# Delta-rule prelude on one core: the second block's Grams behind the first Y, weight tiles loaded one by one

## The chip, the cores and the metric

The kernel runs on one core of a Trainium2 chip. Measured is the device time of one execution in microseconds (us), and the median over several runs is compared. One execution of the kernel before was also taken with the hardware profiler; every row below comes from it. The engines are named as in the profile: TensorE is PE (its weight loads PEld), VectorE is DVE, ScalarE is ACT, GpSimd is POOL, and SyncE (SP) only issues transfers.

## What is computed

Four batches of eight heads run a delta rule over 768 steps with head dimension 48; the result, 3072 tokens of 384 values, goes through two weight matrices with a clipped square between them. 

```python
k_n = k / (np.linalg.norm(k, axis=-1, keepdims=True) + 1e-06)
for t in range(S):
    kt, vt, bt = (k_n[:, :, t], v[:, :, t], beta[:, :, t, None])
    y[:, :, t] = np.einsum('bhd,bhde->bhe', q[:, :, t], state)
    v_old = np.einsum('bhde,bhd->bhe', state, kt)
    state = state + bt[:, :, :, None] * np.einsum('bhd,bhe->bhde', kt, vt - v_old)
...
h = x @ w_in                                   # (3072, 384) @ (384, 2048)
g = np.where(h >= 1, h, np.where(h <= -1, 0.0, (h + 1) ** 2 / 4))
return g @ w_out                               # (3072, 2048) @ (2048, 384)
```

## The kernel before, in words

**Blocks.** The 768 steps are cut into 12 chunks of 64. Two chunks make a pair G (`NS` = 6 pairs), and one chunk of all 32 heads is a block g of 32 triangular 64×64 problems, two heads stacked on the 128 partitions (`NU` = 16 columns of units). For each block the kernel forms the Gram of its keys (`gram_k`, or `gram_first` for the first two), solves (I + A)⁻¹ and gets the output Y and the new state.

**The solve.** For blocks 0 and 1 the diagonal 16×16 parts are inverted on VectorE, one problem per lane (`lanes16`, `solve16`, `unlanes16`, lines 348 to 419); TensorE then joins 16s to 32s (`merge16_a`, `merge16_b`) and 32s to 64s (`merge32_a`, `merge32_b`, lines 431 to 512), `chain_u` applies the inverse to the values, and `first_y` forms the first block's Y. Each of these steps is a batch of small matmuls and then evictions, and waits for the one before it.

**The Grams.** `gram_first(g)` (line 255) does not compute 64×64 Grams but three 32×32 quarters of each, 96 matmuls; its main part leaves the diagonal quarters in PSUM as VectorE reads them, and `below` lets ScalarE copy the third. `gram_k` (line 244) computes whole 64×64 Grams in 32 matmuls. Every one of these matmuls is of type f32 and runs in two passes: the trace shows a weight load and a matmul for each pass. `gram_q(g)` (line 274, 32 matmuls) forms the products of keys and queries; its `evict` is four ScalarE copies onto `WQ`, and GpSimd masks them.

**The weights.** `w_in` and `w_out` come in 16 tiles (`wt`, 768 KB each), loaded by `weight_loads` from SP's queue, the first eight (`SOON`) at the start. The loaded words have to be taken apart: `parts` (line 188) is two ScalarE instructions for each tile (lines 192, 194), `words` (line 198) one VectorE instruction. The second matmul of an item needs its tile whole.

**The order.** The engines run their own lists in order, and the order in which the Python code issues work is that list. From line 686 the prelude is written out by hand: both `gram_first`, both `gram_q`, `hold(KEEP)` (line 675: matmuls on zeros whose result nobody reads, 13 of 256 columns, 26 passes), VectorE's solve of block 0, the merges by `step`, which may put `hold` matmuls (`HEAT`) ahead of a step's evictions, then `first_y`. The generator `bg` (`aside`) carries VectorE's solve of block 1; `pu` and `wu` carry `parts` and `words`.

**The item loop** (from line 916) takes one weight tile at a time for a pair: `up` (x @ w_in into `h`, line 751), ScalarE's and VectorE's activation (lines 904, 932, 940), and `down` (line 770). The pair G = 0 starts with block 0 alone, while block 1 is still in its merges. Tables say what is done between the items: `FIRST`, `OPEN`, `SECOND`, `STEADY` give the slot of each step of the chain in units of half items, `BACK`, `GAIT` and `PACE` how many steps of `bg`, `pu` and `wu` follow each half item.

The queue order at the start is: SP issues the K and Q tiles of both blocks (ScalarE's queue takes six of them), weight tiles 0 and 1, the KV tiles of both blocks and weight tiles 2 to 7.

Of the kernel before, what the change touches and what calls it, by code (L numbers as in the profile page):

```python
# [23 lines left out]
KEEP = 13  # L24
# [10 lines left out]
def delta_rule_moe(ctx: ExitStack, tc: tile.TileContext, kqa, kqb, kv, beta, w, out):  # L35
# [56 lines left out]
    def first_w():  # L92
        tiles = [(g, i) for g in range(2) for i in range(NT)]
        for t in tiles:
            WK[t] = sb.tile([P, NV, C], F32, name="WK", bufs=4)
            WQ[t] = sb.tile([P, 2, NV, C], F32, name="WQ", bufs=4)
        for g, i in tiles:
            nc.sync.dma_start(out=WK[g, i][0:D], in_=kqb[g, i][0:D, 0])
            nc.scalar.dma_start(out=WK[g, i][C:C + D], in_=kqa[g, i][:, 0])
        for g, i in tiles:  # L100
            nc.sync.dma_start(out=WQ[g, i][0:C, 1], in_=kqb[g, i][:, 2])
            (nc.sync if g else nc.scalar).dma_start(out=WQ[g, i][C:C + D, 0], in_=kqa[g, i][:, 1])
# [12 lines left out]
    first_w()
# [671 lines left out]

    FIRST = {'ln': [9.5, 9.5, 10.0, 11.0, 10.0, 10.5, 10.5], 'so': [11.0, 15.0], 'un': [15.5, 15.5, 17.0, 17.0], 'va': [12.0, 15.5], 'vb': [20.0, 19.5], 'r': [16.0], 'm': [17.5, 17.5, 19.0, 19.0], 'kt': [18.0], 'K': [20.0, 20.5], 'T': [21.5, 22.0, 23.0, 23.5, 24.5, 25.0, 25.5], 'Q': [28.5, 29.0]}
    OPEN = {'M': [6.0, 7.0, 7.5, 8.0, 1.0], 'I': [8.5, 9.5, 10.0, 10.5, 2.0, 9.0, 13.0, 14.0], 'X': [1.5, 2.0, 2.5, 4.0, 4.0, 6.5, 6.5, 6.5], 'L': [10.5, 13.5, 4.5], 'W': [23.5, 0.5]}
    SECOND = {'ln': [-6.0, -6.0, -6.0, -5.5, -5.0, -5.5, -5.0], 'so': [-5.0, 4.0]}  # L790
# [1 line left out]
    PACE = [1, 1, 0, 0, 1, 0, 1, 0, 1, 0, 1, 0, 1, 0, 1, 0, 1, 0, 0, 1, 2, 0, 1, 0, 1, 0, 1, 1]
# [1 line left out]
    GAIT = [0, 1, 0, 1, 1, 2, 1, 1, 0, 4, 1, 1, 1, 2, 1, 0, 2, 2, 0, 1, 0, 0, 1, 1, 1, 2]
# [204 lines left out]
```

## Time and profile before

| | |
|---|---|
| median of 3 runs | 610.52 us (610.04 to 611.68) |
| profiled execution | 610.52 us, its span 608.8 us |
[...]
| TensorE matmul busy | 572.8 us, 94% of the span |
| TensorE weight loads | 476.5 us, 78%, beside the matmuls |
| VectorE | 433.0 us, 71% |
| ScalarE | 337.4 us, 55% |
| GpSimd | 61.6 us, 10% |
| the chain that ended last | TensorE 53%, "issue" 27%, VectorE 14%, ScalarE 3% |

The busy shares are means over the whole span. A busy TensorE may be at either clock, and its start is unlike its steady part: in the first two of 40 slices of the span TensorE is 60% and 70% busy, in most later ones over 90%. "Issue" is time in which an engine waited for nothing that the profile shows.

### The profile page before, as it was taken

How to read it: one execution, taken by the hardware profiler on the slowest of the kernel's cores; microseconds unless marked ns; L12 is line 12 of the kernel's file. 1: busy time of each engine (PE TensorE's matmuls, PEld its weight loads, DVE VectorE, ACT ScalarE, POOL GpSimd, SP SyncE). 2: the span in 40 equal slices, each digit the busy share in tenths (PEclk: the TensorE clock that was granted, in tenths of full speed). 3: DMA queues.
4: the chain of work that ended last, by engine and by line, in shares of the span. 5: the costliest groups of instructions: out<-in, count | busy, mean ns of one | idle time of the engine just before them, and what ended most of it. 6: DMA issues, size and time to landing. Idle time of an engine off the chain costs nothing.

```text
span 608.8 us, 19694 instructions
## 1 busy us (share of the span) xinstructions
PE 572.8 (94%) x8572; PEld 476.5 (78%) x8572; DVE 433.0 (71%) x942; ACT 337.4 (55%) x621; POOL 61.6 (10%) x91
## 2 busy tenths in 40 slices
PE   6788897999899999899998999998999999999996
PEld 5666564567677787788887888987888888898995
DVE  7358979995989987779965689955789955433332
ACT  3537883628467577457365547376546375454442
POOL 5054001300004000003000003000003000000000
PEclk8577998999999999999999999999999999999998
DMA  7928322002142000153000332000431000010001
GB/s 234 408 54 309 139 81 90 2 27 56 39 145 90 2 28 2 48 162 89 9 22 2 110 111 79 27 4 2 123 97 53 1 3 13 18 52 1 2 0 52
DMA packets 20646, 42.37 MB, mean 70 GB/s; under 512 B 4336, under 2 KB 9440, under 8 KB 20560
## 3 DMA queue, kind: packets, MB, share of 16 engines
q1 hardware_dynamic: 19440, 40.03, 20.8%
q8 instruction: 67, 1.10, 0.7%
q10 hardware_dynamic: 544, 0.79, 0.5%
q0 software_dynamic: 576, 0.30, 0.3%
q14 instruction: 19, 0.16, 0.1%
HBM read 34.31 MB, written 4.72 MB: 64 GB/s over the span
## 4 chain that ended last, share of the span: by engine, by line
PE 53%; issue 27%; DVE 14%; ACT 3%; DMA 0%; POOL 0%; SPq 0%; POOLq 0%; ACTq 0%; DVEq 0%
PE o L770 18%; PE h L754 17%; PE ch L238 7%; PE h L751 3%; DVE pr L463 2%; DVE A L465 2%; PE ch L586 2%; PE ch L486 2%; PE o L677 1%; DVE wt L204 1%; DVE A L331 1%; DVE s L940 1%; DVE wt L213 1%; DVE GG L242 1%; PE h L263 1%
## 5 line engine op out<-in xcount | busy, mean ns | idle before, releaser
L754 PE MATMUL h<-xb,wt 128*128 128x512 f32 x720 | 182.7, 398 | 1.9 <-DVE s L940 1.6
L770 PE MATMUL o<-wt,ghi 128*128 128x384 f32 x680 | 182.4, 352 | 0.0
L754 PEld LDWEIGHTS h<-xb,wt 128*128 128x128 f32 x720 | 132.6, 188 | 29.5 <-DVE s L940 2.3
L770 PEld LDWEIGHTS o<-wt,ghi 128*128 128x128 f32 x680 | 121.7, 188 | 9.8 <-issue 1.0
L770 PE MATMUL o<-wt,glo 128*128 128x384 f32 x352 | 120.1, 353 | 0.0
L940 DVE SCALAR_TENSOR_TENSOR s<-s,h 128x512 f32<-128x512 f32 (+1 forms) x89 | 58.7, 659 | 58.5 <-ACT s L932 58.1
L899 ACT CAST ghi<-s 128x512 fp32r<-128x512 f32 x80 | 49.7, 621 | 89.9 <-DVE s L940 74.7
L904 ACT ACTIVATE s<-h,half 128x512 f32<-128x512 f32 (+1 forms) x89 | 59.5, 669 | 59.4 <-PE h L754 49.8
L900 DVE TENSOR_TENSOR glo<-s,ghi 128x512 fp32r<-128x512 f32 x80 | 55.1, 689 | 43.6 <-ACT ghi L899 40.6
L770 PEld LDWEIGHTS o<-wt,glo 128*128 128x128 f32 x352 | 65.7, 188 | 3.0 <-DVE glo L900 0.3
L465 DVE TENSOR_TENSOR A<-A,pr 128x30 f32<-128x30 f32 (+9 forms) x150 | 55.1, 368 | 5.2
L932 ACT ACTIVATE s<-s 128x512 f32<-128x512 f32 (+1 forms) x89 | 54.9, 617 | 2.3
L463 DVE TENSOR_TENSOR pr<-A 128x30 f32<-128x30 f32 (+9 forms) x150 | 52.5, 350 | 3.1
L293 POOL TENSOR_SCALAR_AFFINE_SELECT WQ<-WQ 64x512 f32<-64x512 f32 x48 | 34.4, 717 | 161.7 <-ACT WQ L285 159.3
L751 PE MATMUL h<-xb,wt 128*128 128x256 f32 (+1 forms) x144 | 42.2, 430 | 1.8 <-DVE glo L940 1.1
L751 PEld LDWEIGHTS h<-xb,wt 128*128 128x128 f32 x144 | 26.9, 194 | 13.7 <-issue 3.8
L547 ACT COPY SU<-ch 64x384 f32<-64x384 f32 x44 | 20.8, 472 | 16.2 <-PE ch L238 15.5
L586 PEld LDWEIGHTS ch<-WQ,SU 112*64 112x64 f32 x704 | 22.0, 138 | 9.2 <-issue 8.1
L586 PE MATMUL ch<-WQ,SU 112*64 112x64 f32 (+1 forms) x704 | 23.4, 224 | 5.1 <-issue 5.1
L632 DVE TENSOR_TENSOR SU<-ch,SU 48x384 f32<-48x384 f32 x40 | 22.2, 555 | 7.3 <-PE ch L238 6.7
L285 ACT COPY WQ<-ch 64x512 f32<-64x512 f32 x42 | 24.4, 581 | 4.0 <-PE ch L238 3.3
L335 POOL TENSOR_SCALAR_AFFINE_SELECT A<-A 128x1024 f32<-128x1024 f32 x5 | 6.8, 1357 | 195.5 <-ACT y L300 163.5
(167 smaller groups left out, 653.4 us busy)
## 6 DMA issues: line engine op xcount, KB each, us to landing
wt<-in_w_dram SPq DMA_DIRECT2D x16, 768.0 KB, 10.6
KV<-in_kv_dram SPq DMA_DIRECT2D x24, 384.0 KB, 4.6
out_dram<-wx SPq DMA_DIRECT2D x21, 192.0 KB, 2.9
WQ<-in_kqb_dram SPq DMA_DIRECT2D x24, 128.0 KB, 2.7
WK<-in_kqb_dram SPq DMA_DIRECT2D x24, 96.0 KB, 3.5
WQ<-in_kqa_dram SPq DMA_DIRECT2D x22, 96.0 KB, 2.9
WK<-in_kqa_dram SPq DMA_DIRECT2D x20, 96.0 KB, 3.5
xb<-stg SPq DMA_DIRECT2D x60, 32.0 KB, 2.0
```

The costliest lines, as they stand in the source:

```text
L238: nc.tensor.matmul(tiles[i][dst:dst + l.shape[-1], v], l, r, start=True, stop=True)
L463: nc.vector.tensor_tensor(out=pr, in0=A[:, 0:n, j:j + 1].broadcast_to([P, n, m]), in1=A[:, j:j + 1, j + 1:32].broadcast_to([P, n, m]), op= ...
L465: nc.vector.tensor_tensor(out=A[:, 0:n, j + 1:32], in0=A[:, 0:n, j + 1:32], in1=pr, op=ALU.add)
L586: nc.tensor.matmul(yy[tk:tk + C, v // NP, v % NP], SF[rows, u:u + C], w_[rows, h, v, :], start=True, stop=True)
L751: nc.tensor.matmul(h[:, cols(bs)], W32[f][:, 0, k * P:(k + 1) * P], X32[:, k, cols(bs)], start=(k == 0), stop=(k == 2))
L754: nc.tensor.matmul(h[:, cols(bs)], WT[f][:, 0, x, k * P:(k + 1) * P], XB[G][:, y, k, cols(bs)], start=(n == 0), stop=(n == 8))
L770: nc.tensor.matmul(oacc[G, k], x[:, k * P:(k + 1) * P], y, start=(new and n == 0), stop=(left[G, b] == 0 and n == len(passes) - 1))
L899: nc.scalar.copy(out=ghi[:, c], in_=s[:, c])
L900: nc.vector.tensor_tensor(out=glo[:, c], in0=s[:, c], in1=ghi[:, c], op=ALU.subtract)
L904: nc.scalar.activation(out=out, in_=in_, func=AF.Relu, bias=bias, scale=scale)
L932: nc.scalar.activation(out=s[:, c], in_=s[:, c], func=AF.Square)
L940: nc.vector.scalar_tensor_tensor(out=s[:, c], in0=s[:, c], scalar=1.0, in1=h[:, c], op0=ALU.min, op1=ALU.max)
```

## The change

1. `gram_first` is called for block 0 alone, and block 1 gets `gram_k(1)`, issued between `first_y`'s matmuls and its evictions, into the PSUM banks `START[4:6]`. That is 64 matmuls of two passes less. The diagonal quarter that `lanes16(1)` reads is then copied by GpSimd inside the block `GG` (a new first step of `lanes16(1)`).
2. `gram_q(1)` moves from the prelude into the item loop, slot 2.5 (`OPEN["q"]`).
3. `hold(KEEP)` becomes 7 matmuls of 512 columns (14 passes) instead of 13 of 256; `HEAT` has one hold matmul ahead of `merge16_a`'s evictions, as before, none ahead of `merge16_b`'s, and one after `chain_u`'s matmuls.
4. `first_w` takes one block; at the start only block 0's K, Q, beta, KV and block 1's K are loaded. Block 1's Q, beta and KV and the K of block 2 come later.
5. `mark(f)` allocates weight tile f and lets ScalarE copy one element into it, so that the tile's load waits for that ScalarE instruction. The tiles 0 to 7 are loaded behind eight such marks.
6. `parts` runs for three tiles before `merge16_b` instead of two, and the tables `BACK`, `FIRST`, `OPEN`, `SECOND`, `PACE`, `GAIT` have other numbers.

```diff
-KEEP = 13
+KEEP = 7
...
+    def mark(f):
+        RAW[f] = const.tile([P, 2, 2 * DM], F32, name=f"wt{f}")
+        nc.scalar.copy(out=RAW[f][0:1, 0, 0:1], in_=half[0:1, 0:1])
+        weight_loads(f, f + 1)
+
+    first_w(0)
+    first_q(0)
...
     load_beta(0)
-    weight_loads(0, 2)
     load_kv(0)
-    load_kv(1)
-    weight_loads(2, SOON)
+    first_w(1)
...
+        if g:
+            F["G", 1] = GG[:, 1, :, 32:64]
+            for r in (0, C):
+                nc.gpsimd.tensor_copy(out=GG[r:r + 32, 1, :, 32:64], in_=GG[r:r + 32, 1, :, 0:32])
+            yield
...
-    HEAT = [1, 1, 0, 0, 0]
-    BACK = [0, 7, 0, 1, 2, 4, 1, 3, 0, 0, 5, 5, 1, 8, 1, 0, 13]
+    HEAT = [1, 0, 0, 0, 1]
+    BACK = [1, 0, 3, 7, 5, 2, 1, 3, 0, 1, 2, 2, 6, 5, 2, 0, 9]
...
-    ends = [gram_first(0), gram_first(1)]
+    below = gram_first()
     nc.gpsimd.memset(SF, 0.0)
-    load_beta(1)
     run(ln[0], 1)
     b16 = block16(0)
-    run(b16, 1)
+    run(b16, 2)
     run(ln[0], 1)
     run(b16)
     clear()
-    ends[1][0]()
-    ends[0][1]()
-    late_q = [gram_q(0)()]
-    late_q.append(gram_q(1)())
-    hold(KEEP)
+    mark(0)
+    below()
+    mark(1)
+    end = gram_q(0)
+    hold(KEEP, 512)
     run(ln[0])
-    ends[1][1]()
-    run(pu, 2 * HOLD)
+    end = end()
+    load_beta(1)
+    mark(2)
+    run(pu, 2)
+    mark(3)
+    run(pu, 2)
+    first_q(1)
+    mark(4)
     run(solve16(0))
     run(unlanes16(0))
     step(merge16_a, HEAT[0], ((norm16(0), 9), (sv[0], 1)))
+    run(pu, 2)
     step(merge16_b, HEAT[1])
+    mark(5)
+    load_kv(1)
     step(merge32_a, HEAT[2], ((sv[0], 1),))
-    late_q[0]()
+    end()
     step(merge32_b, HEAT[3], ((pu, 1), (wu, 1)))
-    load_k(2)
+    mark(6)
     step(chain_u, HEAT[4], ((pu, 1), (wu, 1)))
-    first_y()()
+    y = first_y()
+    spare[:] = START[4:6]
+    k1 = gram_k(1)
+    y()
+    mark(7)
+    k1()
     rest_beta()
     run(pu, 1)
-    run(bg, 2)
+    load_k(2)
     load_kt(3)
     load_q(2)
     nc.gpsimd.memset(SF[:, 2 * NU * D:], 0.0)
-    late_q[1]()
...
+            at(pe, G, OPEN["q"][0], one(gram_q, 1))
```

What this does to the lists of TensorE and ScalarE is shown at three places.

TensorE, from the start to the first merge, the kernel before (L140 the warm-up, L263 `gram_first`, L238 `gram_q`, L677 the hold, L428 `merge16_a`; x2 is two matmuls):

```order
L140 MATMUL o_121<-warm 128x128 x6
L263 MATMUL ch<-WK 32x32 x96
L263 MATMUL h<-WK 32x32 x96
L238 MATMUL o_383<-WQ,WK 64x64 x2
L238 MATMUL o_384<-WQ,WK 64x64 x2
...
L238 MATMUL o_421<-WQ,WK 64x64 x2
...
L677 MATMUL o_160<-wt_153,warm 128x256 x13
L428 MATMUL ch<-XT,wt_150 64x16 x2
```

and after the change (L269 `gram_first`, L244 `gram_q`, L684 the hold, L435 `merge16_a`):

```order
L146 MATMUL o_97<-warm 128x128 x6
L269 MATMUL ch<-WK 32x32 x96
L244 MATMUL h<-WQ,WK 64x64 x32
L684 MATMUL o_136<-wt_129,warm 128x512 x7
L435 MATMUL o_387<-XT,wt_126 64x16 x2
```

The second `gram_first` and the second `gram_q` are gone from ahead of the hold, and the hold's matmuls are twice as wide.

TensorE behind `chain_u`, after the change (L568 `first_y`, L244 on `WK` alone `gram_k(1)`, L770 the first `h`); before, `first_y` follows `chain_u` directly and the first `h` follows `first_y`:

```order
L684 MATMUL o_136<-wt_129,warm 128x256
L568 MATMUL ch<-WQ,wt_126 64x64 x2
...
L568 MATMUL ch<-WQ,KV 48x64 x4
L244 MATMUL o_659<-WK 64x64 x2
...
L770 MATMUL h<-xb 128x256 x3
```

A hold matmul now stands ahead of `first_y`, and the 32 matmuls of `gram_k(1)` between `first_y` and the first item.

ScalarE from block 0's `below` to the third tile's `parts`, after the change (L119 the marks; L273 `below`; L287 `gram_q(0)`'s evictions; L198 and L200 `parts`, of the tiles wt_254, wt_259 and wt_320, which are weight tiles 0, 1, 2; L444 `merge16_a`'s eviction):

```order
L119 COPY wt_254<-half 1x1
L273 COPY GG<-ch 32x16x32 x2
L119 COPY wt_259<-half 1x1
L287 COPY WQ<-h 64x512 x4
L119 COPY wt_320<-half 1x1
L198 ACTIVATE wt_254<-wt_254,floor 128x768
L200 ACTIVATE wt_254<-wt_254 128x768
L119 COPY wt_325<-half 1x1
L198 ACTIVATE wt_259<-wt_259,floor 128x768
L200 ACTIVATE wt_259<-wt_259 128x768
L119 COPY wt_334<-half 1x1
L444 COPY xb<-o_387 128x128
```

The marks of tiles 2, 3 and 4 stand behind `gram_q(0)`'s evictions and between the `parts` of tiles 0 and 1. Before, ScalarE had eight copies of `gram_q` in this place and the loads of all eight tiles had been issued from the start.

## Rows read from the trace of the kernel before

**Rows 1.** Busy time by stretch: stretch, length, PE, PEld, DVE, ACT, POOL, PEclk, DMA, GB/s
```profile
20.40:33.30 12.90, 10.64 (x144) 8.84 (x140) 0.00 (x1) 9.02 (x15) 0.29 (x1) 0.70 0.98 349
...
48.00:98.60 50.60, 43.82 (x807) 31.53 (x807) 43.70 (x103) 38.15 (x72) 9.32 (x13) 0.96 0.43 160
98.60:608.80 510.20, 494.50 (x6796) 414.74 (x6796) 362.57 (x754) 278.30 (x513) 34.67 (x45) 0.99 0.16 46
```

**Rows 2.** Chain of waits, first 50 us: start us, length us, what
```profile
20.70 2.26 issue
...
24.51 7.64 PE o L677 x26
32.15 0.16 PE ch L428 x2
...
42.29 0.58 issue
...
43.87 2.66 PE o L561 x86
...
48.00 2.04 PE h L751 x4
```

**Rows 3.** VectorE's timeline, 17 to 34 us: start, length, instruction, idle before and releaser
```profile
17.81 1.10 DVE L412 STREAM_TRANSPOSE XT<-xb 128x512 f32<-128x512 f32 x1
...
19.69 0.69 DVE L418 COPY wt<-xb 32x256 f32<-32x256 f32 x2
33.30 0.61 DVE L242 COPY xb<-h 64x128 f32<-64x128 f32 x2 [12.92 <-PE h L428]
```

**Rows 4.** TensorE's timeline, first 21 us
```profile
10.31 2.93 PE L263 MATMUL h<-WK 48*32 48x32 f32 x128 [2.86 <-issue]
16.78 1.39 PE L263 MATMUL h<-WK 48*32 48x32 f32 x45 [3.54 <-issue]
18.10 2.08 PE L238 MATMUL o<-WQ,WK 48*64 48x64 f32 x66
```

**Rows 5.** DMA queues, 13.2 to 16.8 us: packets, MB, share of 16 engines
```profile
q1 hardware_dynamic: 417, 1.44, 99.0%
q8 instruction: 1, 0.02, 1.6%
```

**Rows 6.** DMA queues, 78.4 to 82 us
```profile
q1 hardware_dynamic: 70, 0.33, 22.2%
q8 instruction: 1, 0.02, 1.8%
```

**Rows 7.** The hold's line alone, two stretches: length, PE, PEld, PEclk, DMA, GB/s
```profile
24.40:27.90 3.50, 3.46 (x8) 2.83 (x9) 0.50 1.01 410
27.90:32.20 4.30, 4.25 (x19) 3.35 (x18) 0.97 1.03 301
```

**Rows 8.** TensorE's timeline at 111 us, `gram_q` in a later pair
```profile
110.75 1.16 PE L238 MATMUL ch<-WQ,WK 48*64 48x64 f32 x64
```

**Rows 9.** ScalarE's timeline, first 48 us
```profile
6.01 0.20 ACT L153 ACTIVATE root<-half 128x1 f32<-128x1 f32 x1
...
20.11 2.39 ACT L285 COPY WQ<-o 64x512 f32<-64x512 f32 x4 [5.59 <-PE o L238]
...
29.66 0.98 ACT L192 ACTIVATE wt<-wt,floor 128x768 int32<-128x768 uint8 x1
30.54 0.89 ACT L194 ACTIVATE wt<-wt 128x768 f32<-128x768 f32 x1
...
42.15 0.48 ACT L539 COPY KV<-h 128x384 f32<-128x384 f32 x1 [1.01 <-PE h L238]
```

**Rows 10.** VectorE's timeline at 58 us, a Gram's two copies
```profile
57.80 1.39 DVE L242 COPY GG<-ch 64x512 f32<-64x512 f32 x2
```

**Rows 11.** GpSimd's timeline at 36 us
```profile
35.94 1.27 POOL L503 COPY XT<-XT 32x512 f32<-32x512 f32 x2 [15.26 <-DVE XT L452]
```

**Rows 12.** DMA issues of the page: KB each, us to landing
```profile
wt<-in_w_dram SPq DMA_DIRECT2D x16, 768.0 KB, 10.6
```

More of the change, by code (lines that the diff above doesn't have):

```diff
@@ L90, in load_q, with first_w, first_q @@
             nc.sync.dma_start(out=x[C:C + D, 0], in_=kqa[g, i][:, 1])
[L92 to L102, printed above, removed]
+    def first_w(g):
+        qs = (nc.sync, nc.sync if g else nc.scalar)
+        for i in range(NT):
+            WK[g, i] = sb.tile([P, NV, C], F32, name="WK", bufs=4)
+            WQ[g, i] = sb.tile([P, 2, NV, C], F32, name="WQ", bufs=4)
+            qs[0].dma_start(out=WK[g, i][0:D], in_=kqb[g, i][0:D, 0])
+            qs[1].dma_start(out=WK[g, i][C:C + D], in_=kqa[g, i][:, 0])
+    def first_q(g):
+        qs = (nc.sync, nc.sync if g else nc.scalar)
+        for i in range(NT):
+            qs[0].dma_start(out=WQ[g, i][0:C, 1], in_=kqb[g, i][:, 2])
+            qs[1].dma_start(out=WQ[g, i][C:C + D, 0], in_=kqa[g, i][:, 1])
     def load_kv(g, q=nc.sync):
@@ L110, in weight_loads @@
         for f in range(n0, n1):
-            RAW[f] = const.tile([P, 2, 2 * DM], F32, name=f"wt{f}")
+            if f not in RAW:
+                RAW[f] = const.tile([P, 2, 2 * DM], F32, name=f"wt{f}")
             nc.sync.dma_start(out=RAW[f].bitcast(I32), in_=w.bitcast(I32)[:, f])
-    first_w()
+    def mark(f):
+        RAW[f] = const.tile([P, 2, 2 * DM], F32, name=f"wt{f}")
+        nc.scalar.copy(out=RAW[f][0:1, 0, 0:1], in_=half[0:1, 0:1])
+        weight_loads(f, f + 1)
+    first_w(0)
+    first_q(0)
     beta_sb = const.tile([P, NS, 32], F32, name="beta_sb")
@@ L251, in evict, with gram_first @@
             for k, r in enumerate((0, C)):
-                copy(ONE[0][min(g // 2, 2)][k] if g > 1 else g, GG[r:r + C, g % 2, NV:NU], ts[1][C - r:2 * C - r])
+                copy(g > 1 and ONE[0][min(g // 2, 2)][k], GG[r:r + C, g % 2, NV:NU], ts[1][C - r:2 * C - r])
         return evict
-    def gram_first(g):
+    def gram_first():
         d, e = (ps.tile([P, NU, 32], F32, **acc()) for _ in range(2))
-        F["G", g] = d
+        F["G", 0] = d
         for o, c, t in ((0, 0, d), (32, 32, d), (32, 0, e)):
@@ L261, in gram_first @@
                 for tk, ft, _, h in pairs:
-                    k = WK[g, u // NV][ft:ft + D, u % NV, :]
+                    k = WK[0, u // NV][ft:ft + D, u % NV, :]
                     nc.tensor.matmul(t[tk + o:tk + o + 32, u], k[:, o:o + 32], k[:, c:c + 32], start=True, stop=True)
-        def evict():
-            F["G", g] = GG[:, g, :, 32:64]
-            nc.scalar.copy(out=F["G", g], in_=d)
         def below():
             for r in (32, C + 32):
-                nc.scalar.copy(out=GG[r:r + 32, g, :, 0:32], in_=e[r:r + 32])
-        return evict, below
+                nc.scalar.copy(out=GG[r:r + 32, 0, :, 0:32], in_=e[r:r + 32])
+        return below
     def gram_q(g):
@@ L786, in delta_rule_moe @@
     pe, fill = {}, {}
[L788 to L790 removed]
+    FIRST = {'ln': [9.5, 9.5, 9.5, 10.5, 10.0, 10.5, 10.5], 'so': [10.5, 15.5], 'un': [15.5, 15.5, 17.5, 17.5], 'va': [11.5, 14.0], 'vb': [19.0, 20.0], 'r': [15.5], 'm': [17.5, 17.5, 18.5, 18.5], 'kt': [19.0], 'K': [19.5, 20.5], 'T': [21.5, 22.0, 22.5, 23.5, 24.5, 25.0, 26.0], 'Q': [26.5, 29.0]}
+    OPEN = {'M': [6.5, 7.0, 7.5, 8.0, 1.0], 'I': [8.5, 9.5, 10.0, 10.5, 2.0, 9.0, 11.5, 13.5], 'X': [1.5, 2.5, 4.0, 5.0, 7.0, 7.0, 7.5, 7.5], 'L': [10.5, 12.0, 4.5], 'q': [2.5], 'W': [22.5, 0.5]}
+    SECOND = {'ln': [-6.0, -6.0, -5.5, -6.0, -5.5, -5.0, -5.5], 'so': [-4.5, 5.5]}
     STEADY = dict(ln=[-5.5, -4.5, -4.5, -4.5, -3.5, -2.5, -2.0], so=[-1.5, 5.5], un=[5.5, 6.0, 7.0, 9.5], va=[5.0, 5.5], vb=[11.0, 13.0], r=[6.5], m=[8.0, 9.0, 9.0, 10.5], kt=[2.5], K=[10.0, 11.0], T=[11.5, 12.0, 12.5, 13.0, 13.5, 14.0, 15.0], Q=[18.0, 17.0])
[L792 removed]
+    PACE = [2, 0, 0, 0, 0, 2, 1, 0, 0, 0, 2, 0, 0, 0, 1, 1, 0, 0, 0, 0, 2, 0, 1, 1, 1, 0, 1, 1]
     HOT = []
[L794 removed]
+    GAIT = [1, 0, 0, 0, 4, 1, 0, 2, 1, 1, 2, 0, 0, 2, 0, 2, 0, 1, 0, 0, 0, 1, 2, 2, 1, 1]
     def at(where, G, t, *x):
```

## The prediction

> **What bounds the kernel now.** I read first the busy time of each engine by stretches [rows 1], then the chain of waits over the first 50 us [rows 2], then the timelines of VectorE and TensorE at the places that the chain names, and last the DMA queues there. In [rows 1] the reader is to see that the last stretch, 510.2 us long, is TensorE's (494.5 us busy). The diff leaves its code alone but for two tables, so what the change is worth lies ahead of 98.6 us. Of that, 48.0 us pass before the first `h` matmul of the item loop [rows 2]. In them VectorE, once its solve is done, has 12.90 us with no work at all [rows 1], and [rows 3] give the end of that: the eviction of `merge16_a`, 12.92 us after VectorE's own last copy.
>
> Who was late? `merge16_a` needs `XT`, which VectorE had written by 17.81 + 1.10 = 18.91 us [rows 3], but TensorE works in order and came to it at 32.15 us, after 7.64 us of hold matmuls [rows 2]. Ahead of the hold stand the Grams, both `gram_q` and three pieces called "issue": 2.86 and 3.54 us [rows 4] and 2.26 us [rows 2], together 8.66. So this stretch is bound by TensorE's queue of work that VectorE's chain doesn't need: the second block's Grams, its `gram_q`, the hold.
>
> **What the "issue" pieces are.** TensorE waits there for nothing that its program names. They stand some 256 instructions apart: 128 passes, each a weight load and a matmul, run between the first two [rows 4]. In the second piece the instruction queue q8 moved one packet of 0.02 MB while data queue q1 filled 99.0% of the DMA engines [rows 5]; in a stretch with q1 at 22.2% q8 moved one packet as well [rows 6], and no such piece stands there. I take them for fetches of the program that stand behind the weight tiles' data.
>
> **The change, part by part.** Terms are differences to the profiled execution: a span of 608.80 us and 610.52 us in all, which is also the median of the three runs; 1.72 us lie around the span.
>
> *1. The idle time of VectorE.* Out of the way of `merge16_a` go `gram_first(1)` (192 passes), `gram_q(1)` (64) and two of the three fetches; 64 passes come back later as `gram_k(1)`. If TensorE is through before VectorE, VectorE runs on: its copies end at 19.69 + 0.69 = 20.38 us [rows 3], and `merge16_a`, started at 18.9, needs 33.30 − 32.15 = 1.15 us, which is over by then. Term: **−12.92**.
>
> *2. Is TensorE through?* Of `gram_first(1)`'s 192 passes 128 + 45 ran behind the first edge [rows 4], so 19 ahead of it; these places now belong to `gram_q(0)`, nine matmuls of its 32. The other 23 (46 passes) follow once the fetch is there, at 10.31 us if it is as late as now, and 66 such passes took 2.08 us [rows 4]: 1.4 us, to 11.7. Then come 14 hold passes of 512 columns. [...] The clock rose 3.5 us into the hold [rows 7]; with the same here 4 passes are slow and 10 fast: 11.7 + 3.4 + 4.5 = 19.6 us. That is 0.7 us after `XT` stands, and VectorE goes on at 19.6 + 1.15 = 20.75 instead of 20.38. Term: **+0.4**. Ends: nothing (the fetch early), and, with the clock low throughout, 11.7 + 12.0 + 1.15 = 24.85, that is +4.5.
>
> *3. The hold pass ahead of `first_y`.* `HEAT` moves one matmul (two passes of 256, 0.43 each at the low clock) in front of `first_y`, where TensorE stands for 0.58 us [rows 2]. Term **+0.3**, from 0 to +0.9. The one behind `merge16_b`'s matmuls goes; VectorE and ScalarE evict meanwhile, so nothing.
>
> *4. `gram_k(1)`.* 64 passes between `first_y` and the first `h`. TensorE is free there from 43.87 + 2.66 = 46.53 to 48.00 [rows 2], 1.47 us while ScalarE evicts; at the 2.08 us per 66 passes of [rows 4] it takes 2.0. Term **+0.5**; 0 at the high clock (64 passes in 1.16 us [rows 8]), +2.0 if nothing hides it.
>
> *5. The marks.* Eight ScalarE copies of one element; the nearest row is `root`, 0.20 us [rows 9]. They fall into idle stretches of ScalarE, such as the 1.01 us ahead of the `chain_u` eviction [rows 9]: nothing, with 1.6 us as the other end. What they delay are the loads of tiles 2 to 7, which now start behind the WQ evictions and the unpacking of earlier tiles. What waits for a late tile is told with the third rival.
>
> *6. Work that moves into the first 50.6 us of the loop,* where TensorE is 43.82 and VectorE 43.70 us busy [rows 1]. Two VectorE copies of the Gram (1.39 us [rows 10]) and two GpSimd copies of its diagonal (1.27 [rows 11]) now stand ahead of block 1's solve. ScalarE gets `gram_q(1)`'s four evictions (2.39) for the one unpacking (0.98 + 0.89 = 1.87) that the prelude does more, net 0.52 [rows 9]. TensorE's 64 passes (1.16) fit in its 6.8 us of idle time. I take the other three as paid in full, since VectorE's chain of block 1 ends this stretch: 1.39 + 1.27 + 0.52 = **+3.2**. Ends: 0, if they lie beside others, and +5, if each also delays the next.
>
> *7. Tables.* `BACK`, `PACE`, `GAIT` and the due times reorder work inside that stretch. No row prices an order: **0**, from −1.5 to +1.5, which is 3% of its length either way.
>
> Sum: −12.92 + 0.4 + 0.3 + 0.5 + 3.2 = −8.5. The first `h` matmul comes at 48.0 − 11.7 = 36.3 us, and the time is 610.5 − 8.5 = **602.0 us**. With all ends good it is 596, with all bad 614; they won't coincide.
>
> [...] The three pieces of 8.66 us stand in a stretch of full DMA engines with a q8 packet in it [rows 5]. [...]
>
> **Rivals.**
> - *The pieces stay, for a cause that has nothing to do with fetches.* TensorE then saves its matmuls alone: 192 passes at 2.93 us per 128 [rows 4] are 4.4, `gram_q(1)` is 2.0, and 14 × 512 hold columns in place of 26 × 256 cost 0.6 more. The hold ends at 32.15 − 4.4 − 2.0 + 0.6 = 26.35, VectorE goes on at 27.5, and the gain is 33.3 − 27.5 = 5.8, less the 4.0 of terms 3 to 6: 608.7 us. Against it: the pieces follow the count of instructions [rows 4]. Chance 0.05. [...]
> - *The low clock lasts through the hold* (term 2's far end). For it: ahead of the hold stand stalls and short matmuls, as before. Against it: before, the hold's own passes were enough. 602.0 + 4.1 = 606.1 us. Chance 0.11.
> - *Slower: the weight tiles come late.* With L from issue to landing, tile 0 (mark at some 10.2 us, behind `block16`) lands at 10.2 + L, its unpacking (1.87) frees mark 3, and tile 3 lands at 12.1 + 2L. The first half of tile 3's unpacking (0.98) stands in ScalarE's order ahead of `chain_u`'s eviction, due at 42.15 − 11.7 = 30.4. If 13.1 + 2L passes that, TensorE and VectorE wait behind it. At the 10.6 us that is the median now [rows 12] this costs 13.1 + 21.2 − 30.4 = 3.9 us, 606 in all; the time passes 610.5 at L = 12.9, and at L = 15 it is 602.0 + 12.7 = 614.7. For it: the loads start later. Against it: the 10.6 us are of tiles queued behind each other; q1 moved 1.44 MB in 3.6 us [rows 5], which makes 2 us for a tile's 0.79 MB, and at most four are now on their way at once. Chance 0.05.
>
> **How the numbers follow.** The forecast has a chance of 0.73, the rivals have 0.21, and 0.06 is left for a loop stretch that gives back more than +5 (607 to 610 us). The range of 598.3 to 606.6 takes in the forecast's ends where two or three of them add up, the clock rival and the milder half of the late tiles; it leaves out 0.2. A measurement of this kernel tells 0.3%, 1.8 us, from no change, so faster means under 608.7. Faster: 0.73 + 0.11, and 0.04 of the pieces that stay and the loop that gives back: 0.88. Same: the other 0.07 of these two. Slower: 0.05.
>
> **What would show it.** Right: the first `h` matmul at 34 to 40 us; VectorE's idle time before the eviction of `merge16_a` at most 1.5 us; one "issue" piece over 1 us in the first 25 us instead of three; no unpacking on ScalarE that waits for a weight tile's DMA; 53 to 55 us instead of 50.6 from the first `h` to the wait for `xb<-stg`; and the rest 510 as before. Wrong: three pieces as now (first rival); a granted clock of 0.5 all through the hold (second); ScalarE idle on `wt` loads with `chain_u` behind it (third); or a loop stretch of 58 us or more, which would mean that the prelude's gain was only moved.

## The result: 1.4% faster, and the profile after

The changed kernel takes 602.14 us (median of four runs, 600.59 to 602.78) against 610.28 us of the kernel before in the same series: a ratio of 0.986, 95% interval 0.9833 to 0.9886. Run again beside later experiments it took 602.53 us, ratio 0.9877 (0.9858 to 0.9896); in that second profile the three pieces shown below are 2.83, 3.21 and 1.23 us long instead of 3.20, 2.53 and 0.66, and the first `h` matmul comes at 38.85 us, so differences of some 0.6 us between two profiles tell nothing. The profiled execution has a span of 600.9 us against 608.8, 7.9 us less.

Busy time by stretch of the kernel after, cut at VectorE's last copy of block 0 (21.13), the first `h` matmul (38.27) and the end of the wait before the second block's first 512-wide matmul (91.33); columns as in [rows 1]:

```profile
0.00:21.13 21.13, 16.80 (x347) 11.66 (x347) 16.86 (x64) 11.81 (x22) 9.11 (x19) 0.92 0.78 240
21.13:38.27 17.14, 12.32 (x427) 10.11 (x421) 9.76 (x22) 6.86 (x16) 8.79 (x16) 0.70 0.72 234
38.27:91.33 53.06, 45.52 (x874) 33.68 (x871) 46.66 (x108) 39.01 (x74) 10.49 (x14) 0.93 0.52 181
91.33:600.90 509.57, 494.35 (x6796) 414.26 (x6796) 363.05 (x751) 279.96 (x515) 35.25 (x45) 0.99 0.16 46
```

The first `h` matmul comes at 38.27 us instead of 48.00 (−9.73), the stretch behind it is 53.06 us long instead of 50.58 (+2.48; it ended at 98.58 before), and the rest takes 509.57 instead of 510.22 (−0.65).

VectorE's timeline after, which answers to [rows 3]: the 12.92 us of idle time have become 0.17.

```profile
18.52 1.15 DVE L419 STREAM_TRANSPOSE XT<-xb 128x512 f32<-128x512 f32 x1
...
20.44 0.69 DVE L425 COPY wt<-xb 32x256 f32<-32x256 f32 x2
21.29 0.61 DVE L248 COPY xb<-o 64x128 f32<-64x128 f32 x2 [0.17 <-PE o L435]
```

TensorE's timeline after, which answers to [rows 2, 4]: `gram_q(0)` behind its "issue" piece, the hold, `merge32_b` behind a new piece, `gram_k(1)` behind a short one.

```profile
11.36 0.92 PE L244 MATMUL h<-WQ,WK 48*64 48x64 f32 x45 [3.20 <-issue]
12.21 7.94 PE L684 MATMUL o<-wt,warm 128*128 128x512 f32 x14
...
28.12 0.26 PE L493 MATMUL h<-GG 32*32 32x32 f32 x2 [2.53 <-issue]
...
37.54 0.80 PE L244 MATMUL o<-WK 48*64 48x64 f32 x36 [0.66 <-issue]
```

And what the data queues did around the new piece (the two stretches of the kernel after; the ninth column, 1.04 and 1.00, is the DMA share), beside the merges of the kernel before:

```profile
21.80:25.40 3.60, 2.48 (x130) 2.04 (x129) 3.29 (x11) 1.86 (x5) 1.33 (x3) 1.00 1.04 257
25.40:28.10 2.70, 0.19 (x1) 0.08 (x1) 1.02 (x3) 0.33 (x1) 2.50 (x4) 0.58 1.00 399
```

```profile
33.30:48.00 14.70, 10.97 (x356) 9.00 (x357) 10.08 (x23) 5.80 (x12) 8.22 (x14) 0.67 0.09 24
```

Before, the data queues were nearly empty when the merges ran (share 0.09), and no piece over 0.2 us stood in them. Now the merges run while weight tiles and block 1's KV come in. From `merge16_a`'s eviction to the first `chain_u` matmul it was 39.75 − 33.30 = 6.45 us and is 29.68 − 21.29 = 8.39: 1.94 us more, with the piece of 2.53 us in it. The weight tiles were hardly late for ScalarE: one wait for a tile stands in its list, 1.52 us and off the path, and the page's median time to landing is 6.2 us in place of 10.6 [rows 12]:

```profile
18.14 1.02 ACT L198 ACTIVATE wt<-wt,floor 128x768 int32<-128x768 uint8 x1 [1.52 <-DMA wt<-in_w_dram]
```

```profile
wt<-in_w_dram SPq DMA_DIRECT2D x16, 768.0 KB, 6.2
```

### The profile page after: what moved, and what is told of

The parts are those of the page before. It is cut to its first block, busy times and chain, and to the rows that moved or that the text cites. A ratio compares the mean times of both kernels' runs of the same rounds, so it can differ in the third digit from the quotient of the medians.

```text
span 600.9 us, 19441 instructions
## 1 busy us (share of the span) xinstructions
PE 569.0 (95%) x8432; PEld 469.7 (78%) x8432; DVE 436.3 (73%) x944; ACT 337.6 (56%) x627; POOL 63.6 (11%) x93
## 4 chain that ended last, share of the span: by engine, by line
PE 57%; issue 26%; DVE 13%; ACT 1%; POOL 1%; DMA 1%; POOLq 0%; DVEq 0%; ACTq 0%
PE o L789 20%; PE h L773 17%; PE ch L244 7%; PE h L770 4%; PE ch L593 2%; DVE pr L470 2%; DVE A L472 2%; PE ch L493 2%; PE o L684 2%; DVE wt L210 1%; DVE s L960 1%; DVE XT L480 1%; DVE GG L248 1%; DVE A L333 1%; PE o L244 1%
## 5 line engine op out<-in xcount | busy, mean ns | idle before, releaser
L789 PEld LDWEIGHTS o<-wt,glo 128*128 128x128 f32 x352 | 65.9, 188 | 2.8
L295 POOL TENSOR_SCALAR_AFFINE_SELECT WQ<-WQ 64x512 f32<-64x512 f32 x48 | 35.9, 748 | 162.8 <-ACT WQ L287 160.4
L770 PE MATMUL h<-xb,wt 128*128 128x256 f32 (+1 forms) x144 | 43.4, 439 | 0.5 <-DVE s L960 0.5
L770 PEld LDWEIGHTS h<-xb,wt 128*128 128x128 f32 x144 | 26.6, 195 | 9.9 <-issue 3.8
L287 ACT COPY WQ<-ch 64x512 f32<-64x512 f32 x44 | 25.5, 581 | 10.1 <-PE ch L244 6.5
```

Source lines behind the costliest of these rows:

```text
L770: nc.tensor.matmul(h[:, cols(bs)], W32[f][:, 0, k * P:(k + 1) * P], X32[:, k, cols(bs)], start=(k == 0), stop=(k == 2))
L789: nc.tensor.matmul(oacc[G, k], x[:, k * P:(k + 1) * P], y, start=(new and n == 0), stop=(left[G, b] == 0 and n == len(passes) - 1))
```

## The experiments

The theory that they test, F: TensorE asks for its next block of 256 instructions when it enters the one before, and gets it some 3.7 us later with quiet data queues (no row shows it; the second probe below gives 3.65) and some 6.5 us later with full ones (16.78 − 10.31 = 6.47 [rows 4]). A stall is what is missing to the time that TensorE takes for a block, and an edge is the place where one block ends and the next begins. Of the rivals, N holds that the pieces have nothing to do with the count of instructions, D that fetches are late only behind data, M that the marks bring part of the gain by themselves. Ratios are to the kernel before in the same series.

**The Grams back in front**

```diff
     first_w(1)
+    first_q(1)
...
-    below = gram_first()
+    ends = [gram_first(0), gram_first(1)]
...
     end = gram_q(0)
+    end1 = gram_q(1)
     hold(KEEP, 512)
...
-    k1 = gram_k(1)
```

> The changed kernel with the second block's Grams back in front: gram_first(1) and gram_q(1) ahead of the hold, no gram_k(1), block 1's Q loaded at the start; marks, hold and tables as changed. Theory F: 192 + 64 passes come back (4.4 + 2.0 us) and with them two more block edges with a stall each, 2 to 4 us for the first and 0 to 2 for the second. The hold ends at 29 to 32 us instead of 20.15, VectorE idles 8 to 11 us before merge16_a's eviction; gram_k(1) and the moved work give back some 3 us; time 607 to 611. Rival N (the stalls have nothing to do with the count of instructions): only the matmuls come back, hold end at 26.6 us, VectorE idle 5.5 us, time 604 to 606.

(Block 1's `lanes16` then reads its diagonal quarter from PSUM, without GpSimd's copies.) 613.41 us (608.72 to 614.65 in eight runs), ratio 1.0043 (1.0018 to 1.0068): the whole gain is gone, and more. TensorE's and VectorE's timelines of this kernel:

```profile
10.53 0.74 PE L270 MATMUL h<-WK 48*32 48x32 f32 x19 [2.58 <-DMA WK<-in_kqa_dram]
...
16.74 1.39 PE L270 MATMUL h<-WK 48*32 48x32 f32 x45 [1.57 <-issue]
...
21.94 8.55 PE L684 MATMUL o<-wt,warm 128*128 128x512 f32 x14
```

```profile
31.64 0.61 DVE L249 COPY xb<-h 64x128 f32<-64x128 f32 x2 [10.28 <-PE h L435]
```

The hold ends at 30.5 us and VectorE idles 10.28 us, inside F's range and not 5.5 as N had it. But F's range was met in part by luck: 2.58 us of the idle time are a wait for block 1's K, which is loaded behind block 0's Q and KV and comes late for `gram_first(1)`, and neither theory had it. The two "issue" pieces stand at the edges that F names, 128 passes apart, but they are 0.38 and 1.57 us long; so this run speaks for F by the places more than by the sizes. Nor did the loop give anything back: the stretch behind the first `h` (47.92 us) takes 54.56 us against 53.06. The median lies 2.4 us above the expected range, while three of the eight runs are at 608.7 to 610.0 us; what parts them I leave open. That TensorE's queue ahead of the hold is what VectorE waited for is shown.

**The marks taken out**

```diff
     load_kv(0)
     first_w(1)
+    weight_loads(0, SOON)
...
     def mark(f):
-        RAW[f] = const.tile([P, 2, 2 * DM], F32, name=f"wt{f}")
-        nc.scalar.copy(out=RAW[f][0:1, 0, 0:1], in_=half[0:1, 0:1])
-        weight_loads(f, f + 1)
+        pass
```

> The changed kernel without the marks: weight tiles 0 to 7 are queued on SP at the start, behind block 1's K. Theory F (a block of 256 TensorE instructions is requested when the block before it is entered, and arrives some 3.7 us later with quiet data queues, some 6.5 us with full ones; the stall is what is missing to the time that TensorE takes for a block): the data queues are full from 7 to some 24 us. The first stall, 3.2 us in the changed kernel, grows to 3.5 to 4.5; the stall in merge32_b (2.5 us) shrinks to under 1.2, since its block is requested at 21.8 us and the queues run dry soon after. First h matmul at 36.5 to 38 us, time 600.0 to 602.0. Rival M (the marks themselves bring part of the gain, since early tiles hold up the instruction fetch and block 1's loads): first stall over 5 us or TensorE late for merge16_a by over 2 us, time 604 or more.

603.6 us, ratio 0.9903 (0.9886 to 0.992), between the two forecasts: by the medians 0.2% slower than the changed kernel, by the ratios 0.3 to 0.4%, with intervals that overlap a little. TensorE's timeline:

```profile
29.05 0.26 PE L492 MATMUL h<-GG 32*32 32x32 f32 x2 [2.66 <-issue]
...
51.64 1.97 PE L243 MATMUL ch<-WQ,WK 48*64 48x64 f32 x60 [3.53 <-issue]
```

The expectation missed twice. The first stall is 2.85 us, not 3.5 to 4.5. And I had the queues empty by 24 us, but the loads that follow in SP's order then start early too, and from 24 to 26 us they are full:

```profile
24.00:26.00 2.00, 1.20 (x64) 0.86 (x64) 1.82 (x6) 0.26 (x1) 1.21 (x2) 1.00 1.02 385
```

So the stall in `merge32_b` stays, as F says of full queues. The first `h` comes at 39.47, 1.2 us later than in the changed kernel's first profile and 0.6 later than in its second. The wait of 3.53 us in the loop is no fetch: VectorE's Gram copy ends at 51.54, just before TensorE goes on, as it does behind the 3.3 us that the changed kernel's trace puts down to that copy. VectorE's line here:

```profile
50.15 1.39 DVE L247 COPY GG<-ch 64x512 f32<-64x512 f32 x2
```

**The tiles moved away from the merges**

```diff
     first_q(1)
-    mark(4)
...
     step(merge16_b, HEAT[1])
-    mark(5)
-    load_kv(1)
...
     step(merge32_b, HEAT[3], ((pu, 1), (wu, 1)))
+    mark(4)
+    mark(5)
+    load_kv(1)
     mark(6)
```

> The changed kernel with marks 4 and 5 and block 1's KV loads moved from before and behind merge16_b to behind merge32_b, beside mark 6, so that the data queues run dry between some 23 and 31 us. Theory F: the 2.5 us stall in merge32_b shrinks to under 1.2, and as the tiles now load from 29 us on, the edge in gram_k(1) (0.66 us now) gets a full queue and stalls 1.5 to 3.5 us; the first h matmul stays within 1 us of 38.3, time 600.5 to 603.5. Rival N (the stalls belong to their places and not to the data queues): 2.5 us in merge32_b and 0.7 us in gram_k(1) as now, time 601.5 to 603. Rival L (the tiles come late): ScalarE waits over 1 us for a weight tile and the time passes 603.5.

602.99 us, ratio 0.9893 (0.9879 to 0.9907). This is the sharpest of the runs. The waits of TensorE in the first 60 us have no piece in `merge32_b` any more, and one of 3.3 us instead of 0.66 in `gram_k(1)` (line, waited for, us in total, times, longest):

```profile
PE o L244 <- issue: 3.3, 1, 3.3
PE ch L244 <- DVE GG L248: 3.1, 1, 3.1
PE h L244 <- issue: 3.0, 1, 3.0
```

Two stretches, the first with the block of `merge32_b` on its way, the second with that of `gram_k(1)`; DMA share 0.35 and 0.97:

```profile
21.60:25.40 3.80, 2.68 (x130) 2.12 (x130) 3.45 (x12) 1.92 (x4) 1.49 (x3) 1.00 0.35 88
...
29.80:33.90 4.10, 4.08 (x127) 3.17 (x126) 2.45 (x4) 2.05 (x6) 2.76 (x7) 0.67 0.97 356
```

Not one TensorE instruction was changed; only loads and their marks moved, and the stall moved with them. Rival N falls. From `merge16_a`'s eviction (21.14) to `chain_u` (27.27) it is 6.13 us here against 8.39, so the piece costs 2.26 us on the path. These 2.3 us were lost again 8 us later, and the first `h` came at 38.50.

The instruction queue shows the mechanism directly. In the whole changed kernel q8 moves 66 packets, and TensorE's 2 × 8432 instructions make 65.9 blocks of 256:

```profile
q8 instruction: 66, 1.08, 0.7%
```

In the changed kernel the edge in `merge16_b` is passed at some 21.8 us. From 21.8 to 25.4 us only the data queue moves anything:

```profile
q1 hardware_dynamic: 339, 0.92, 103.9%
```

The packet starts between 25.5 and 25.6 us, 3.7 us behind the edge:

```profile
q8 instruction: 1, 0.02, 63.8%
```

In the kernel with the tiles moved away the same packet starts between 22.4 and 22.5 us, some 0.9 us behind its edge:

```profile
q8 instruction: 1, 0.02, 63.0%
```

So it is the packet itself that is late beside the data. From its start to TensorE's next pass it was 28.12 − 25.5 = 2.6 us.

**No hold**

```diff
-    HEAT = [1, 0, 0, 0, 1]
+    HEAT = [0, 0, 0, 0, 0]
...
-    hold(KEEP, 512)
```

> The changed kernel without hold matmuls: KEEP's seven and HEAT's two are left out (their result is read by nobody). Theory H (the hold is there for the clock alone and costs nothing any more, since merge16_a's eviction waits only 0.17 us for it): granted clock 0.5 from the first stall to the loop, merge16_a and merge16_b 64 passes each in 1.4 to 2.1 us instead of 1.1, merge32_a likewise, time 0.5 to 2 us more: 602.6 to 604. Rival (dead weight): the short merges wait for evictions anyway, time 601.0 to 602.4. Theory F adds: with 16 passes less ahead of merge32_b its edge moves 16 passes further on, and the stall there stays 1 to 2.6 us.

601.56 us, ratio 0.9878 (0.9861 to 0.9896), the same as with it. The granted clock is 0.50 in the merges, and `merge16_a` takes 1.91 us instead of 1.12:

```profile
19.60:24.90 5.30, 4.61 (x134) 4.32 (x134) 3.99 (x13) 2.45 (x6) 0.95 (x3) 0.50 0.99 277
```

```profile
19.69 1.91 PE L435 MATMUL o<-XT,wt 64*64 64x16 f32 x64 [6.78 <-DVE XT L419]
```

But it begins when `XT` is written, so VectorE goes on at 21.68 instead of 21.29. The edge in `merge32_b` stalls 1.06 us:

```profile
28.57 0.26 PE L493 MATMUL h<-GG 32*32 32x32 f32 x2 [1.06 <-issue]
```

The block ahead of it took TensorE some 4.9 us here (from 22.6, an estimate by the count of passes, to 27.5) against 3.8, so by F less of the fetch was left to wait for. The first `h` comes at 38.72. The expectation that the hold is worth 0.5 to 2 us missed, and its rival held: the 7.94 us of hold buy nothing that this profile can show.

**A first probe of the fetch**

```diff
+    PROBE = (6, 34, 36)
...
         h = up(*item)
+        if n in PROBE:
+            t = ps.tile([P, 512], F32, name="ch", bufs=2)
+            for _ in range(192):
+                nc.tensor.matmul(t[0:C, 0:C], warm[0:D, 0:C], warm[0:D, 0:C], start=True, stop=True)
```

> The changed kernel with 192 matmuls of 64 columns on zeros (384 passes, 768 instructions, three blocks) put in at three places of the loop: behind the first matmuls of item 6 (some 55 to 65 us, data queues over 80% full) and of items 34 and 36 (second pair, queues nearly empty). Their result is read by nobody. At 18 ns a pass a block of 128 passes takes 2.3 us. Theory F: with empty queues each full block edge stalls 3.7 less 2.3, that is 1.0 to 1.8 us, two or three edges at each place; with full queues 2.5 to 4.2 us. Rival D (fetches are late only behind data): no stall over 0.3 us at items 34 and 36, 2.5 us or more at item 6. Rival N (no such thing as a fetch stall): none at any of the three.

723.35 us (one run): the probe told nothing of fetches, since a pass took 35.86 us / 384 = 93 ns and a block 12 us:

```profile
63.87 35.86 PE L947 MATMUL ch<-warm 48*64 48x64 f32 x384
```

**The probe again, alternating between halves of the array and slots of the bank**

```diff
+            for m in range(192):
+                a, b = (0, C) if m % 2 else (C, 0)
+                nc.tensor.matmul(t[a:a + C, m // 2 % NV], warm[b:b + D, 0:C], warm[b:b + D, 0:C], start=True, stop=True)
```

> The probe again, with its 192 matmuls (384 passes, three blocks of instructions) alternating between the two halves of the array and between eight slots of the PSUM bank, as the Grams do, so that one need not wait for the other: some 18 ns a pass at the high clock instead of the 93 ns of the first try. Places as before: item 6 (full data queues) and items 34 and 36 (nearly empty ones); the result is read by nobody. Theory F: a block of 128 passes takes 2.3 us, its fetch 3.7 us from the entry of the block before; so 1.0 to 1.8 us of stall at each full block edge with empty queues, two or three edges at a place, and 2.5 to 4.2 us with full ones. Rival D (late only behind data): under 0.3 us at items 34 and 36. Rival N: none at any place.

641.43 us (one run). A pass now took 11.41 / 384 = 29.7 ns, not the 18 that I had expected, so a block lasts 3.8 us, and no stall stands in the probe at any of the three places. All three had quiet data queues (a share of 0.01 to 0.02, item 6 too), so full queues were not tried. What tells is the work behind the last one, 128 passes of which lie in quick merges (TensorE's timeline, then the DMA queues from 252.9 to 256.7 us, where this was the only packet):

```profile
242.28 11.41 PE L948 MATMUL ch<-warm 48*64 48x64 f32 x384
253.63 0.72 PE L493 MATMUL ch<-XT,GG 32*32 32x32 f32 x62
...
254.19 0.58 PE L493 MATMUL ch<-GG 32*32 32x32 f32 x43
256.72 0.37 PE L493 MATMUL ch<-GG 32*32 32x32 f32 x19 [1.94 <-issue]
```

```profile
q8 instruction: 1, 0.02, 1.9%
```

From 253.63 to the stall 62 + 43 and four single passes run, 109 in all; the block was therefore entered 19 passes (0.6 us) earlier, at 253.07, and the next one was there at 256.72. That is 3.65 us with empty data queues, where rival D had none. The packet starts here between 254.0 and 254.1 us, some 1 us behind the edge, and TensorE goes on 2.7 us later:

```profile
q8 instruction: 1, 0.02, 70.9%
```

In full queues it was the 6.47 us above and, in the kernel after, 28.12 − 21.8 = 6.3 (from 11.36 on 45 + 14 + 64 + 2 passes run to `merge16_b`, whose third pass, at 21.8, is the edge). It is no constant. In the changed kernel's second profile VectorE's `XT` copy behind the piece starts at 29.74 us instead of 29.34 and `merge16_a`'s eviction ahead of the edge at 21.02 instead of 21.29, from which I estimate some 7.0 us at the same edge; with the old tables (below) these two start at 29.83 and 22.91, which makes some 5.2.

**gram_q(1) taken out of the loop**

```diff
     k1()
+    gram_q(1)()()
     rest_beta()
...
-            at(pe, G, OPEN["q"][0], one(gram_q, 1))
```

> The changed kernel with gram_q(1) moved out of the loop's slot 2.5 to right behind gram_k(1) in the prelude, its four ScalarE evictions too. Theory P (TensorE's 64 passes and ScalarE's 2.4 us are cheaper in the loop than ahead of its first matmul): first h 1 to 3 us later, the stretch from first h to the end of block 0's items 0.5 to 1.5 us shorter, time 602.5 to 604.5. Rival (the loop's added 2.5 us come from gram_q(1)): stretch 2 us or more shorter, time 600.5 to 602.

609.11 us, ratio 0.9988 (0.9971 to 1.0005): far outside both expectations, with nearly the whole gain lost. The first `h` comes at 43.52, 5.2 us later, of which 1.7 had already passed at `chain_u` (31.41), ahead of the edit; the stretch behind it takes 57.55 us instead of 53.06. GpSimd's timeline of this kernel, then the first step of block 1's solve on VectorE:

```profile
44.09 2.81 POOL L295 TENSOR_SCALAR_AFFINE_SELECT WQ<-WQ 64x512 f32<-64x512 f32 x4 [14.44 <-ACT WQ L287]
46.85 4.22 POOL L136 DMA_DIRECT2D beta_sb<-in_beta_dram  x8
...
51.28 1.26 POOL L364 COPY GG<-GG 32x512 f32<-32x512 f32 x2
```

```profile
52.58 1.05 DVE L366 STREAM_TRANSPOSE A<-GG 128x512 f32<-128x512 f32 x1 [3.83 <-POOL GG L364]
```

and GpSimd's timeline of the changed kernel:

```profile
39.21 2.05 POOL L364 COPY GG<-GG 32x512 f32<-32x512 f32 x2 [6.43 <-DVE GG L248]
```

GpSimd, too, went through its list in order here. Its masks of `gram_q(1)` wait for ScalarE's evictions until 44.09, eight DMA issues stand behind them, and then only come the two copies from which VectorE's solve of block 1 starts: 51.28 instead of 39.21. The stretch behind the first `h` ends 9.7 us later (101.07 instead of 91.33). I had priced TensorE and ScalarE and forgotten this queue. What the copies' place alone costs, without `gram_q(1)` ahead of the first `h`, no run shows.

**The old tables**

```diff
-    BACK = [1, 0, 3, 7, 5, 2, 1, 3, 0, 1, 2, 2, 6, 5, 2, 0, 9]
+    BACK = [0, 7, 0, 1, 2, 4, 1, 3, 0, 0, 5, 5, 1, 8, 1, 0, 13]
```

and `FIRST` and `SECOND` likewise.

> The changed kernel with the tables FIRST, SECOND and BACK of the kernel before (PACE, GAIT and OPEN stay as changed): an order alone, no work more or less. Theory 7 (the tables reorder work inside the loop's first stretch and are worth 0, from -1.5 to +1.5 us): first h as in the changed kernel within 0.5 us, the stretch behind it 51 to 55 us, time 601 to 604. Rival T (the tables carry a part of the gain, since gram_q(1) and the GpSimd copies stand in new places): stretch 56 us or longer, time 605 or more.

611.33 us (606.96 to 616.64), ratio 1.0008 (0.9985 to 1.0031): all of the gain lost, with the first `h` at 38.89 us as early as ever. VectorE's transpose that ends block 1's solve, with the old tables and in the changed kernel:

```profile
67.28 1.06 DVE L419 STREAM_TRANSPOSE XT<-xb 128x512 f32<-128x512 f32 x1
```

```profile
61.88 1.15 DVE L419 STREAM_TRANSPOSE XT<-xb 128x512 f32<-128x512 f32 x1
```

`BACK` counts steps of `bg`. The old one reckons with two steps made in the prelude and one step fewer in all, so here it lags by three. The stretch behind the first `h` is 57.37 us long, the rest 513.84; of the latter's 4 us I have no cause. The expectation missed and its rival T held; which of the three tables does it was not tried.

**Loads early, behind one mark; then a shorter hold; then KV later**

```diff
     mark(0)
+    weight_loads(1, 6)
     below()
-    mark(1)
...
     step(merge32_b, HEAT[3], ((pu, 1), (wu, 1)))
+    hand()
```

`hand()` loads block 1's KV and Q behind a ScalarE mark; marks 2 to 5 and the loads beside them go, and mark 6 stands beside mark 7.

> The changed kernel with its loads rearranged: tiles 0 to 5 are all issued behind mark 0 (some 10.2 us), block 1's KV and Q behind a mark ahead of chain_u's evictions (some 29 us), tiles 6 and 7 behind marks 6 and 7 after first_y. Theory F: TensorE works at the hold from 12 to 20 us and needs few instructions, so the six tiles cost it nothing there; by 22 to 24 us the queues are empty and the stall in merge32_b shrinks from 2.5 to under 1.2 us; the edge in gram_k(1) stays under 1.2 us. First h matmul 1 to 2.5 us earlier than in the changed kernel, time 599.5 to 601.5. Rival M (something else is bad about early tiles, as in the kernel without marks): first h as now or later, 602 to 604.

601.62 us, ratio 0.9863 (0.9841 to 0.9886). The stall in `merge32_b` is gone. But the first one was 4.07 us long in this profile (2.8 to 4.1 in those of kernels with the same start), the hold took 8.55 us and ended at 21.96, and VectorE waited for it:

```profile
DVE xb L257 <- PE o L444: 2.3, 1, 2.3
```

So the first `h` came at 38.71, not earlier: the expectation missed, as the gain in the merges was lost ahead of them and by 1.87 us of "issue" in `gram_k(1)`. With `KEEP = 4`:

> The kernel with rearranged loads, its hold cut from 7 to 4 matmuls of 512 columns (8 passes). In it merge16_a's eviction waited 2.27 us for a hold that ended at 21.9 us. With 6 passes less, at the high clock 0.45 us each, it ends at some 19.2 us, before VectorE's last copies: the wait shrinks to under 0.7 us, first h at 36.5 to 37.5 us instead of 38.71, time 599.5 to 601. Rival C (the clock falls back before the merges and takes the gain): merge16_a's 64 passes in 1.5 us or more, first h at 38 us or later, time 601 to 602.5.

600.57 us, ratio 0.9854 (0.9826 to 0.9883); `merge16_a` is evicted at 20.78 and the first `h` comes at 37.42, as expected. The queues are full again while `gram_k(1)` is fetched (DMA share 0.97 from 31.2 to 36.8 us), and its edge stalls:

```profile
33.91 2.88 issue
36.80 0.69 PE o L253 x30
```

as its chain of waits has it. With `hand()` moved behind `first_y`'s evictions:

> The kernel with rearranged loads and the short hold, its loads of block 1's KV and Q moved from before chain_u's evictions to behind first_y's, beside tiles 6 and 7. In the kernel without that move gram_k(1)'s edge stalled 2.9 us (33.9 to 36.8 us) with the data queues full from 30 us on. Theory F: the queues are empty while that block is fetched, so its stall shrinks to under 1.2 us, first h at 35 to 36.3 us instead of 37.42, time 598 to 600. Rival L (block 1's values and the tiles then come late for the loop): first h early as above, but the stretch behind it 1 to 3 us longer than the 52.59 us of that kernel, time 600 to 602.

602.78 us, ratio 0.9885 (0.9854 to 0.9916). The piece in `gram_k(1)` is gone and the first `h` comes at 35.87 us, the earliest of all; then the K of block 2, which SP issues behind these loads, is 6 us late:

```profile
47.67 0.48 PE L253 MATMUL ch<-WK 48*64 48x64 f32 x4 [6.02 <-DMA WK<-in_kqa_dram]
```

and the stretch behind the first `h` takes 56.48 us, rival L in other clothes. Of the three, the middle one has the lowest median, but its interval overlaps that of the changed kernel: no version is shown to beat it.

## Why the prediction was right, step by step

The forecast of 602.0 us met 602.14, by a sum whose large terms were right. That it met within 0.2 us is luck: two errors, of 2.0 and 1.4 us, nearly cancelled. One sum was off: with all ends bad the terms add up to 613 us, not 614.

- *Terms 1 and 2, VectorE's idle time and the hold* (−12.92 + 0.4 = −12.5): measured 21.29 − 33.30 = −12.0. The hold took 7.94 us, as forecast: 3.4 + 4.5 are four passes of 512 columns at twice the 3.46/8 = 0.43 us of one of 256 at a granted clock of 0.50 and ten at twice the 4.25/19 = 0.22 at 0.97 [rows 7], and in the kernel after the clock was 0.50 from 12.21 to 15.60 us and 1.00 from there to 20.10. It ended at 20.15 instead of 19.6, mainly since the first fetch came at 11.36 and not 10.31. What VectorE lost was not the hold's, which cost it 0.17 us: it was itself 0.75 us later than before (21.13 for 20.38). The Gram experiment shows the mechanism, with 10.28 us of idle time when the Grams come back, 2.58 of them a late load.
- *The fetches* (part of term 1, "two of the three fetches" go): here the prediction stopped short. The first piece stayed, 3.20 us, as forecast. But every block of 128 passes has an edge (66 packets of q8 for 65.9 blocks), and I did not follow the count into the merges: the third one falls into `merge32_b`, where the loads now keep the queues full. 2.53 us of "issue", some 2 on the path, were in no term. The sign of one piece in the first 25 us was met only because the second began at 25.6. Also, "behind the weight tiles' data" was half of it: the probe shows 3.65 us with nothing else on the queues.
- *Term 3, the hold pass ahead of `first_y`* (+0.3): nothing. From `chain_u`'s first matmul to `first_y`'s main part it was 43.87 − 39.75 = 4.12 us and is 33.79 − 29.68 = 4.11.
- *Term 4, `gram_k(1)`* (+0.5): +0.4, as 38.27 − 36.36 = 1.91 us lie between `first_y`'s end and the first `h`, against 1.47. Of that, 0.66 is a fetch that the term did not have; without it the gap would be no longer than before, so the size is right and the working is not.
- *Term 5, the marks* (nothing): they cost nothing that shows. By the medians the kernel without them is 0.2% slower, which I had not priced at all.
- *Term 6, the loop's first stretch* (+3.2): +2.48, and +1.64 in the repeated run (52.22 us). The size was near, the working was not. GpSimd's copies (2.05 us there, not 1.27) end at 41.26 and are covered by VectorE's unpacking, which lasts to 42.07; they cost only if something stands ahead of them on GpSimd, which the `gram_q(1)` run shows.
- *Term 7, the tables* (0, −1.5 to +1.5): the rest gave −0.65. Yet the bound was wrong as a statement on tables: with the old ones the gain is lost. The new order is what keeps the loop from giving the prelude's gain back.

Of the rivals, the first (the pieces have another cause) fell with the run in which only loads moved. The second fell by the hold's 7.94 us, which it had at 12.0; and the run without a hold, at a granted clock of 0.50 in the merges, was no slower (601.56 us). The third did not come: 6.2 us to landing, and one wait of 1.52 us off the path, though the prediction had named no such wait at all as a sign of being right. Terms 1 to 4 and the stall make 38.27 − 48.00 = −9.73 where −11.7 was forecast, 2.0 us of gain too few; the loop gave back 0.7 us less than forecast and the rest gained 0.65, 1.4 us too many. These nearly balance.

What an edge cost went with the time that TensorE took for the block ahead of it: in the second probe the blocks of 3.8 us show no stall (quiet queues) and one of 1.7 us (253.07 to 254.78) was followed by 1.94 us; in the kernel after, with full queues, one of 3.8 us (21.8 to 25.6) was followed by 2.53.

## What to carry to other kernels

Where TensorE runs many tiny matmuls, count its instructions as a load of their own: at the edges followed here the next 256 were there 3.65 us (quiet queues, the second probe) or, in part by estimate, 5.2 to 7.0 us (full ones) after TensorE had entered the block before, and where that block took it less time, a stall stands. With the Grams' 256 passes back in front VectorE idled 10.28 us, 2.58 of them for a late load. To start large loads while TensorE has long matmuls took one stall away, the 2.53 us in `merge32_b`, in the three kernels with rearranged loads, but none of them is shown to be faster. Look at what an engine off the path holds in its queue before moving work to it: with GpSimd's two copies behind masks and DMA issues, and `gram_q(1)` ahead of the first `h`, nearly all that the change had gained was lost (609.11 us). And when a prelude becomes shorter, the hand-set order of the loop behind it has to be set anew, or the loop takes the gain, as with the old tables (611.33 us).

## What was not expected of the hardware

- Matmuls of 48 rows and 64 columns on one place of the array, all with the same output, took 93 ns a pass; alternating between the halves of the array and between slots of the bank, 29.7 ns. The clocks differ (next point), so not all of the factor is the place; the parts were not separated.
- The granted clock during these slow passes, with TensorE busy in all records, was 0.59; during the alternating ones it was 1.00.

```profile
63.90:99.60 35.70, 35.70 (x385) 35.64 (x384) 4.88 (x13) 2.59 (x4) 0.81 (x2) 0.59 0.01 1
```

```profile
63.50:74.80 11.30, 11.30 (x385) 11.28 (x384) 4.91 (x13) 2.60 (x5) 0.82 (x2) 1.00 0.02 4
```

- Without any hold the merges ran at a granted clock of 0.50, and the kernel was as fast (601.56 us beside 602.14).
- With full data queues (the kernel after, share 1.04) the packet of TensorE's next instructions started 3.7 us behind the edge, with quiet ones (the second probe) some 1 us; from its start to the next pass it was 2.6 and 2.7 us.
